# A convolution and a two-layer MLP on one core: the second tap sum from superblock 10 on, and a checked softmax with a general version behind it

## The chip, the cores and the metric

The kernel runs on one core of one Trainium2 chip. The time is that of the device in microseconds. Before the change it is 746.78 us, the median of three runs (745.8 to 747.22).

The core's engines are named as in the profile: PE (TensorE, matmuls), PEld (its weight loads), DVE (VectorE), ACT (ScalarE), POOL (GpSimd) and SP (SyncE, which here only issues DMAs).

## The reference

x is 8 x 4096 x 192 (float32), weight_gen is 8 x 4096 x 8 x 7, w_in is 192 x 2048 and w_out is 2048 x 192. A softmax over seven weights for each token and each of eight heads gives the taps of a causal convolution along the sequence. The result goes through a matmul, a tanh-shrink and a second matmul.

```
w = weight_gen - np.max(weight_gen, axis=-1, keepdims=True)
w = np.exp(w)
w = w / (np.sum(w, axis=-1, keepdims=True) + 1e-09)
...
out = np.einsum('bshk,bskhg->bshg', w, x_unf)      # x_unf: tokens s-6 .. s
...
h = x @ w_in
g = h - np.tanh(h)
return (g @ w_out).astype(np.float32)
```

## The kernel before

The 32768 tokens are cut into 32 superblocks of 1024, numbered 0 to 31. Partition p of a superblock holds the eight consecutive tokens 8p to 8p + 7. One superblock passes these stages, spread over the time of several superblocks:

- **Softmax, four superblocks ahead.** SP loads the weights (L120), ACT takes the exponential in place without subtracting a maximum (L169), DVE sums it in two halves (`softmax_sum`, L183), takes the reciprocal (L198) and scales (L229). From superblock 28 on there is none of this left to do.
- **Taps, two superblocks ahead.** POOL multiplies x by the seven taps (L299). Taps 0 to 3 go to the tile `pa` in two instructions, taps 4 to 6 to `pb` in one. `products` issues the first, and `rest` the `pb` product at f = 3 or later. DVE takes over taps 0 and 1 of the last token of each partition, and in superblocks 9 to 14 of the last two tokens (`HELP`, the function `help`, L250 and L251). An entry (n, f) of `HELP[m]` says that DVE works for superblock m in superblock n after f tile f.
- **Tap sums by DMA.** A DMA that adds (L236, issued by POOL) adds `pb` to taps 0 to 2 of `pa`. That leaves four parts. For a superblock in `TWO_SUMS`, a second such DMA adds taps 2 and 3 of `pa` to taps 0 and 1, which leaves two. `second_sum` issues it after the first products of the next superblock.
- **Transposes, one superblock ahead.** PE transposes and adds up the remaining parts in PSUM against an identity (L384), 24 matmuls for each part, and ACT copies the result to `convT` (L410).
- **First matmul, f = 0 to 15.** Six matmuls for each of 16 tiles of 128 hidden units (L427) into a PSUM tile `ph`, of which there are three buffers. ACT takes the tanh (L440), and DVE subtracts it and writes `gt` (L441), which frees `ph`.
- **Second matmul, one superblock behind.** `out_stream` (L495) works through token blocks in pairs of matmuls, ACT copies each block to `out_sb` (L514), and SP stores a superblock at a time (L518). The last superblock has its own version, `gemm2_last` (L538), with an ACT copy (L551), a DVE add (L552) and a store for two blocks (L554).

The order on each engine is the order of the program text (a manual schedule). A plan fixes, for each superblock, how many pairs of the second matmul follow each f tile (`pairs`), and behind which tile the two transposes stand (`t1` for chunk 2, `t2` for chunks 0 and 1). `DOUBLE` has the larger transposes behind f = 11 and the smaller behind f = 15, `STEADY` behind f = 13 and 14:

```
STEADY = dict(pairs=(5, 11, 0, 16, 4, 12, 6, 10, 0, 6, 10, 8, 8, 8, 8, 16), t1=(14, 8), t2=(13, 0), scale=14, sums=(1, 13))
...
DOUBLE = dict(pairs=(4, 12, 0, 16, 0, 16, 5, 11, 0, 5, 11, 6, 10, 0, 16, 16), t1=(15, 4), t2=(11, 4), scale=15, sums=(1, 10))
DOUBLE_IN = (4, 5, 6, 7, 8, 9, 10, 11)
```

So superblock n with the plan `DOUBLE` transposes superblock n + 1. On SP, the load of x for superblock m is ordered behind the first product of superblock m - 1 on POOL (from superblock 10 on), and everything behind it in the queue of SP waits too.

## Time and profile before

| | |
|---|---|
| Median of three runs | 746.78 us (745.8 to 747.22) |
| Span of the profiled execution | 743.4 us; its whole time is not listed |
| Granted clock of PE, mean | 0.995 |
| PE, busy | 722.3 us (97%) |
| DVE, busy | 687.4 us (92%) |
| POOL, busy | 654.5 us (88%) |
| ACT, busy | 638.8 us (86%) |
| Chain that ended last | PE 92%, DVE 5% |
| Superblock 9 / superblock 15 | 22.67 us / 21.86 us |
| Landing of a first tap sum / a second, median | 9.5 us / 7.2 us |

Times inside the profile count from the start of its span. Busy time counts an engine's own work; a DMA-issuing instruction of POOL or SP is listed under the engine that issues it. In lists by time the first number is the start, the second the length; the bracket at the end gives the idle time before it and what ended that.

### The profile page before, as it was taken

What the parts mean: (1) busy time and instruction counts of PE and PEld (TensorE: products, weight loads), DVE (VectorE), ACT (ScalarE), POOL (GpSimd) and SP (SyncE); (2) the same over time, 40 slices, a digit from 0 to 9 for tenths busy, and PEclk for the clock granted to TensorE, in tenths of its full rate; (3) what the DMA queues carried; (4) which work ended last, traced back from release to release, by engine and by line L of the source; (5) the groups of instructions that cost most, each with busy time, mean ns of one, the idle gap of its engine ahead of it and who ended that gap; (6) DMA issues with size and microseconds to landing.
All of it is one profiled execution on the core that took longest, in us unless ns stands there. A gap on an engine that the chain in (4) does not pass through costs nothing.

```text
span 743.4 us, 30037 instructions
## 1 busy us (share of the span) xinstructions
PE 722.3 (97%) x13616; PEld 556.5 (75%) x13616; DVE 687.4 (92%) x723; ACT 638.8 (86%) x872; POOL 654.5 (88%) x163
## 2 busy tenths in 40 slices
PE   3899999999999999999999999999999999999997
PEld 2477777778777777777777777777777777877777
DVE  7999899999999999999999999999999999988893
ACT  4888888888888888989889999898998989888882
POOL 7999999999999999999999999999999999991000
PEclk9899999999999999999999999999999999999999
DMA  8925367766567668878777977877887877776112
GB/s 236 245 46 161 135 172 185 195 179 149 124 183 184 183 185 224 210 199 203 166 202 209 236 186 204 178 195 205 221 209 195 192 181 194 193 149 110 45 45 86
DMA packets 34269, 130.06 MB, mean 175 GB/s; under 512 B 4591, under 2 KB 9439, under 8 KB 30174
## 3 DMA queue, kind: packets, MB, share of 16 engines
q0 software_dynamic: 19424, 51.12, 40.4%
q1 hardware_dynamic: 14718, 77.03, 27.6%
q8 instruction: 106, 1.74, 0.9%
q14 instruction: 21, 0.17, 0.1%
HBM read 54.52 MB, written 25.17 MB: 107 GB/s over the span
## 4 chain that ended last, share of the span: by engine, by line
PE 92%; DVE 5%; ACT 1%; issue 1%; DMA 1%; SPq 0%; DVEq 0%
PE ph L427 43%; PE obank L495 43%; PE pc L384 4%; DVE gt L441 3%; PE po L538 1%; ACT th L440 1%; DVE pa L299 1%; DMA wg_t<-in_weight_gen_dram 1%; DVE zsum L183 0%; SPq L134 0%; ACT convT L402 0%; DVE obank L211 0%; DVE pa L251 0%; DVE pb L299 0%; SPq L144 0%
## 5 line engine op out<-in xcount | busy, mean ns | idle before, releaser
L441 DVE TENSOR_TENSOR gt<-ph,th 128x1024 bf16<-128x1024 f32 x512 | 601.6, 1217 | 33.4 <-ACT th L440 23.2
L440 ACT ACTIVATE th<-ph 128x1024 f32<-128x1024 f32 x512 | 512.1, 1025 | 69.2 <-PE ph L427 60.3
L427 PE MATMUL ph<-convT,w_in 64*128 64x512 bf16 x3072 | 415.1, 379 | 5.3 <-DVE gt L441 3.3
L495 PEld LDWEIGHTS <-gt 64*128 64x128 bf16 x7936 | 355.6, 94 | 80.6 <-issue 6.3
L495 PE MATMUL obank<-w_out,gt 64*128 64x192 bf16 x7936 | 408.0, 243 | 0.9 <-issue 0.8
L299 POOL TENSOR_TENSOR pa<-x_t,wsm 128x2688 bf16<-128x2688 f32 (+3 forms) x68 | 338.9, 5232 | 0.2
L299 POOL TENSOR_TENSOR pb<-x_t,wsm 128x4608 bf16<-128x4608 f32 (+2 forms) x33 | 283.8, 8601 | 0.7 <-ACT wsm L221 0.5
L427 PEld LDWEIGHTS <-w_in 64*128 64x128 bf16 x3072 | 163.0, 94 | 86.0 <-issue 18.3
L514 ACT ACTIVATE out_sb<-obank 128x192 f32<-128x192 f32 x248 | 81.3, 328 | 11.2 <-PE obank L495 10.3
L410 ACT ACTIVATE convT<-pc 128x1024 bf16<-128x1024 f32 (+1 forms) x62 | 50.1, 810 | 2.9 <-PE pc L384 2.7
L236 POOL DMA_DIRECT2D pa<-pb x28 | 36.0, 1284 | 13.7 <-POOL pb L299 9.1
L384 PEld LDWEIGHTS <-pa 64*128 64x128 bf16 x2064 | 41.5, 100 | 6.8 <-DVE pa L299 1.1
L236 POOL DMA_DIRECT2D pa<-pa x21 | 34.7, 1651 | 9.6 <-DMA pa<-pb 8.9
L384 PE MATMUL pc<-ident,pa 64*128 64x64 bf16 x1968 | 41.2, 191 | 1.8 <-POOL pa L299 0.9
L183 DVE TENSOR_REDUCE zsum<-wg_t 128x32 f32<-128x224 f32 (+1 forms) x61 | 23.6, 387 | 2.9 <-ACT wg_t L169 2.9
L169 ACT ACTIVATE wg_t<-wg_t 128x448 f32<-128x448 f32 x32 | 18.2, 570 | 6.3 <-DMA wg_t<-in_weight_gen_dram 6.2
L251 DVE TENSOR_TENSOR pa<-x_t,ph 128x384 bf16<-128x384 f32 x34 | 18.8, 554 | 2.0 <-DVE ph L250 0.3
L229 DVE TENSOR_TENSOR wsm<-wg_t,pc 128x448 f32<-128x448 f32 x27 | 16.8, 621 | 2.5
L198 DVE RECIPROCAL pc<-zsum 128x64 f32<-128x64 f32 x27 | 14.9, 550 | 0.0
L384 PE MATMUL pc<-ident,pb 64*128 64x64 bf16 x216 | 4.9, 206 | 9.0 <-POOL pb L299 9.0
L384 PEld LDWEIGHTS <-pb 64*128 64x128 bf16 x288 | 6.3, 106 | 9.5 <-POOL pb L299 9.0
L538 PE MATMUL po<-w_out,gt 64*128 64x192 bf16 x256 | 11.2, 243 | 0.0
(27 smaller groups left out, 56.8 us busy)
## 6 DMA issues: line engine op xcount, KB each, us to landing
x_t<-in_x_dram SPq DMA_DIRECT2D x31, 1344.0 KB, 7.9
pa<-pb POOLq DMA_DIRECT2D x28, 1152.0 KB, 9.5
out_dram<-out_sb SPq DMA_DIRECT2D x31, 768.0 KB, 3.9
pa<-pa POOLq DMA_DIRECT2D x21, 768.0 KB, 7.2
wg_t<-in_weight_gen_dram SPq DMA_DIRECT2D x32, 224.0 KB, 7.1
x_t<-in_x_dram SPq DMA_DIRECT2D x1, 768.0 KB
w_out<-in_moe_w_out_dram POOLq DMA_DIRECT2D x1, 768.0 KB, 9.5
out_dram<-out_sb SPq DMA_DIRECT2D x4, 192.0 KB, 3.0
```

The source lines that it names most:

```text
L183: nc.vector.reduce_sum(out=zsum_of[n][:, j0 * H : j1 * H], in_=e_of[n][:, j0:j1].rearrange("p j h k -> p (j h) k"), axis=AX.X,)
L236: return nc.gpsimd.dma_start(out=out.rearrange("p k j d -> p k (j d)"), in_=in_.rearrange("p k j d -> p k (j d)"), accum_op=mybir.AluOpTyp ...
L251: nc.vector.tensor_mul(pa[:, 0:KH, j, :].rearrange("p k (h g) -> p k h g", h=H), bass.AP(tensor=x_v.tensor, offset=x_v.offset + j * D, ap= ...
L299: return eng.tensor_mul(prod(k0, k1)[:, :, j0:j1].rearrange("p k j (h g) -> p k (j h) g", h=H), bass.AP(tensor=x_v.tensor, offset=x_v.offs ...
L384: nc.tensor.matmul(pc[r][:, col : col + R] if home else pc[:, r, col : col + R], lhsT=prods[c][gi][r * R : (r + 1) * R, 2 * j : 2 * j + 2] ...
L410: last_conv[0] = nc.scalar.activation(out=out, in_=pc[:, :, 0:cols].rearrange("p r (cj t) -> p r cj t", t=R), func=ACT.Copy,)
L427: nc.tensor.matmul(ph[:, r, :], lhsT=w_in[r * R : (r + 1) * R, c, f * P : (f + 1) * P], rhs=convT[r * R : (r + 1) * R, c, :], start=(c == ...
L440: last_act[0] = nc.scalar.activation(out=th[:], in_=ph_f, func=ACT.Tanh)
L441: last_sub[0] = nc.vector.tensor_sub(gt[:], ph_f, th[:])
L495: mm = nc.tensor.matmul(po[:, 0:D], lhsT=g_of[n][f][r * R : (r + 1) * R, col : col + P], rhs=w_out[r * R : (r + 1) * R, f, :], start=(r == ...
L514: last_act[0] = nc.scalar.activation(out=out_sb[:, j, :], in_=po[:, 0:D], func=ACT.Copy)
L538: nc.tensor.matmul(po[:, r, 0:D], lhsT=g_of[n][f][r * R : (r + 1) * R, col : col + P], rhs=w_out[r * R : (r + 1) * R, f, :], start=(f == 0 ...
```

## The change

The change has three parts.

1. Superblocks 10, 11 and 12 join `TWO_SUMS`, and `DOUBLE_IN` ends at 8, so superblocks 9, 10 and 11 follow the plan `STEADY`.
2. `HELP` loses the second token of superblocks 12, 13 and 14. POOL's first product for them has 2688 columns in place of 2304.
3. All softmax sums are kept in one tile, `zall`. DVE takes the largest and the smallest of each half of it (in superblocks 28 to 31), compares them with 1e30 and 1e-18, and reduces the outcome to one integer, after a DMA has brought the 128 partitions' answers into one row. Every engine loads that integer and branches. If a sum was out of range, a general version in loops (with the maximum subtracted) computes everything anew. The store of the last two token blocks stands behind the branch, on both ways.

```
-    TWO_SUMS = (13, 14, 15, ... 31)
+    TWO_SUMS = (10, 11, 12, 13, 14, 15, ... 31)
...
-    HELP = {...} | {9: ((7, 3), (6, 12)), 10: ((8, 3), (7, 12)), 11: ((9, 3), (8, 12)), 12: ((10, 3), (9, 12)), 13: ((11, 3), (10, 12)), 14: ((12, 3), (11, 12))}
+    HELP = {...} | {9: ((7, 3), (6, 12)), 10: ((8, 3), (7, 12)), 11: ((9, 3), (8, 12))}
...
+    STORES = {1: 0, 3: 2, 5: 4}
+    LAST_STORE = {7: 6}
+    SUM_MAX, SUM_MIN = 1e30, 1e-18
+    CHECK = {(28, 14): (0,), (29, 14): (1,), (30, 14): (2,), (31, 8): (3,)}
...
-            zsum_of[n] = wgpool.tile([P, J * H], FP32, name="zsum")
+            zsum_of[n] = zall[:, n * J * H : (n + 1) * J * H]
...
+    def sums_piece(i):
+        w = NTOT * J * H // 2
+        if i < 4:
+            op = ALU.max if i < 2 else ALU.min
+            nc.vector.tensor_reduce(ends[:, i : i + 1], zall[:, i % 2 * w : (i % 2 + 1) * w], AX.X, op)
+        elif i == 4:
+            nc.vector.tensor_scalar(ends[:, 0:2], ends[:, 0:2], SUM_MAX, None, op0=ALU.is_le)
+        elif i == 5:
+            nc.vector.tensor_scalar(ends[:, 2:4], ends[:, 2:4], SUM_MIN, None, op0=ALU.is_ge)
+        elif i == 6:
+            nc.vector.tensor_mul(fine[:], ends[:, 0:2], ends[:, 2:4])
+            nc.sync.dma_start(out=fine_row[:], in_=fine[:])
+        else:
+            nc.vector.tensor_reduce(flag[:], fine_row[:], AX.X, ALU.min)
...
-        if j % 2 == 1:
-            nc.sync.dma_start(...)
+        if j in STORES:
+            store_last(j)
...
-    DOUBLE_IN = (4, 5, 6, 7, 8, 9, 10, 11)
+    DOUBLE_IN = (4, 5, 6, 7, 8)
...
+            for piece in CHECK.get((n, f), ()):
+                sums_piece(piece)
...
+    for piece in (4, 5, 6):
+        sums_piece(piece)
     gemm2_last(0, 0, J)
     out_pairs(NFT)
     gemm2_last(0, J, NFT)
     for j in range(1, J):
+        if j == 4:
+            sums_piece(7)
         gemm2_last(j)
+    sched.__exit__(None, None, None)
...
+    good = nc.values_load(flag[:], min_val=0, max_val=1)
+    with tc.If(good < 1, preferred_fallthrough_block=False):
+        with tc.For_i(0, B) as b:
+            carry = xpool.tile([P, HALO + J, D], FP32, name="x_t")
+            nc.vector.memset(carry[0:1, 0:HALO, :], 0.0)
+            with tc.For_i(0, NSB) as s:
+                general(b * NSB + s, carry)
+    STORES.update(LAST_STORE)
+    store_last(J - 1)
```

`general` (not shown) does one superblock from the loads to the store. With the inputs of the reference every sum is in range, and it is never entered.

More of the change, by code (lines that the diff above doesn't have):

```diff
@@ L13 @@
 AX = mybir.AxisListType
+ALU = mybir.AluOpType
 @with_exitstack
@@ L45 @@
     PART = (2, 3)
-    TWO_SUMS = (13, 14, 15, 16, 17, 18, 19, 20, 21, 22, 23, 24, 25, 26, 27, 28, 29, 30, 31)
+    TWO_SUMS = (10, 11, 12, 13, 14, 15, 16, 17, 18, 19, 20, 21, 22, 23, 24, 25, 26, 27, 28, 29, 30, 31)
     AHEAD = 4
@@ L49 @@
     EXTRA = (5, 9, 11, 13)
-    HELP = {n: ((n - 2, 3),) for n in (4, 5, 6, 7, 8, 9, 10, 11, 12, 13, 14, 15, 16, 17, 18, 19, 20, 21, 22, 23, 24, 25, 26, 27, 28, 29, 30, 31)} | {9: ((7, 3), (6, 12)), 10: ((8, 3), (7, 12)), 11: ((9, 3), (8, 12)), 12: ((10, 3), (9, 12)), 13: ((11, 3), (10, 12)), 14: ((12, 3), (11, 12))}
+    HELP = {n: ((n - 2, 3),) for n in (4, 5, 6, 7, 8, 9, 10, 11, 12, 13, 14, 15, 16, 17, 18, 19, 20, 21, 22, 23, 24, 25, 26, 27, 28, 29, 30, 31)} | {9: ((7, 3), (6, 12)), 10: ((8, 3), (7, 12)), 11: ((9, 3), (8, 12))}
     LAST_TAP = (4, 5, 6, 7, 8)
     X_LATE = ()
+    STORES = {1: 0, 3: 2, 5: 4}
+    LAST_STORE = {7: 6}
+    SUM_MAX, SUM_MIN = 1e30, 1e-18
+    CHECK = {(28, 14): (0,), (29, 14): (1,), (30, 14): (2,), (31, 8): (3,)}
     ZERO_AT = 8
@@ L83 @@
     once = const.tile([P, 1], FP32, name="once")
+    zall = const.tile([P, NTOT * J * H], FP32, name="zall")
+    ends = const.tile([P, 4], FP32, name="ends")
+    fine = const.tile([P, 2], FP32, name="fine")
+    fine_row = const.tile([1, 2 * P], FP32, name="fine_row")
+    flag = const.tile([1, 1], mybir.dt.int32, name="flag")
     x_of = {}
@@ L197, in softmax_norm @@
         zr_v = bank[:, 512 - J * H : 512]
-        nc.vector.reciprocal(zr_v, zsum_of[n][:])
+        nc.vector.reciprocal(zr_v, zsum_of[n])
         def finish():
@@ L210, in softmax_norm_ramp @@
         zr_v = bank[:, 512 - J * H : 512]
-        nc.vector.reciprocal(zr_v, zsum_of[n][:])
+        nc.vector.reciprocal(zr_v, zsum_of[n])
         if n == 2:
@@ L527, in out_pairs, with store_last @@
             next(pairs)
+    def store_last(j):
+        n = NTOT - 1
+        nc.sync.dma_start(
+            out=out[n * TOK : (n + 1) * TOK, :].rearrange("(p j) e -> p j e", p=P)[:, STORES[j] : j + 1, :],
+            in_=out_of[n][:, STORES[j] : j + 1, :],
+        )
     def gemm2_last(j, f0=0, f1=NFT):
@@ L552, in gemm2_last @@
         nc.vector.tensor_add(out_sb[:, j, :], po[:, 1, 0:D], ot[:])
-        if j % 2 == 1:
-            nc.sync.dma_start(
-                out=out[n * TOK : (n + 1) * TOK, :].rearrange("(p j) e -> p j e", p=P)[
-                    :, j - 1 : j + 1, :
-                ],
-                in_=out_sb[:, j - 1 : j + 1, :],
-            )
+        if j in STORES:
+            store_last(j)
     w_in = const.tile([P, NC, F], BF16, name="w_in")
     w_out = const.tile([P, NFT, D], BF16, name="w_out")
-    ctx.enter_context(tc.manual_schedule())
+    sched = tc.manual_schedule()
+    sched.__enter__()
     def load_w_out():
@@ L773, with general, rows, spread @@
     for j in range(1, J):
+        if j == 4:
+            sums_piece(7)
         gemm2_last(j)
+    sched.__exit__(None, None, None)
+    def general(m, carry):
+        x_t = xpool.tile([P, HALO + J, D], FP32, name="x_t")
+        def rows(p0, p1, r0, r1):
+            first = x.rearrange("b s d -> (b s) d")[bass.ds(m * TOK, 1)]
+            nc.sync.dma_start(
+                out=x_t[p0:p1, r0:r1, :],
+                in_=bass.AP(
+                    tensor=first.tensor,
+                    offset=first.offset + (p0 * J - HALO + r0) * D,
+                    ap=[[J * D, p1 - p0], [D, r1 - r0], [1, D]],
+                ),
+            )
+        rows(0, P, HALO, HALO + J)
+        rows(1, P, 0, HALO)
+        nc.sync.dma_start(out=x_t[0:1, 0:HALO, :], in_=carry[0:1, 0:HALO, :])
+        nc.sync.dma_start(out=carry[0:1, 0:HALO, :], in_=x_t[P - 1 : P, J : J + HALO, :])
+        e_t = wgpool.tile([P, J, H, K], FP32, name="wg_t")
+        nc.sync.dma_start(
+            out=e_t[:],
+            in_=weight_gen.rearrange("b s h k -> (b s) h k")[bass.ds(m * TOK, TOK)].rearrange(
+                "(p j) h k -> p j h k", p=P
+            ),
+        )
+        e_v = e_t[:].rearrange("p j h k -> p (j h) k")
+        zr = wgpool.tile([P, J * H], FP32, name="zr")
+        def spread(v):
+            return v.rearrange("p (n o) -> p n o", o=1).to_broadcast([P, J * H, K])
+        nc.vector.tensor_reduce(zr[:], e_v, AX.X, ALU.max)
+        nc.vector.tensor_sub(e_v, e_v, spread(zr[:]))
+        nc.scalar.activation(
+            out=e_t[:].rearrange("p j h k -> p (j h k)"),
+            in_=e_t[:].rearrange("p j h k -> p (j h k)"),
+            func=ACT.Exp,
+        )
+        nc.vector.reduce_sum(out=zr[:], in_=e_v, axis=AX.X)
+        nc.vector.reciprocal(zr[:], zr[:])
+        nc.vector.tensor_mul(e_v, e_v, spread(zr[:]))
+        total = papool.tile([P, J, D], FP32, name="total", tag="pa")
+        part = papool.tile([P, J, D], FP32, name="part", tag="pa")
+        summed = pbpool.tile([P, J, D], BF16, name="pb")
+        x_v = x_t[:]
+        for k in range(K):
+            to = total if k == 0 else part
+            nc.vector.tensor_mul(
+                to[:].rearrange("p j (h g) -> p (j h) g", h=H),
+                bass.AP(tensor=x_v.tensor, offset=x_v.offset + k * D, ap=[x_v.ap[0], [G, J * H], [1, G]]),
+                e_t[:].rearrange("p j h (k o) -> p k (j h) o", o=1)[:, k].to_broadcast([P, J * H, G]),
+            )
+            if k > 0:
+                nc.vector.tensor_add((summed if k == K - 1 else total)[:], total[:], part[:])
+        prods_of[NTOT] = [[summed[:]]] * NC
+        conv(NTOT, (0, 1), (2,))
+        convT = conv_of.pop(NTOT)
+        out_sb = opool.tile([P, J, D], FP32, name="out_sb")
+        nc.vector.memset(out_sb[:], 0.0)
+        with tc.For_i(0, NFT) as f:
+            w_f = tpool.tile([P, NC, P], BF16, name="w_f", tag="th")
+            nc.sync.dma_start(out=w_f[:], in_=w_in[:, :, bass.ds(f * P, P)])
+            w_o = tpool.tile([P, D], BF16, name="w_o", tag="th")
+            nc.sync.dma_start(out=w_o[:], in_=w_out[:, bass.ds(f, 1), :].rearrange("p o e -> p (o e)"))
+            ph = psum_h.tile([P, 2, HT], FP32, name="ph", tag="ph")
+            for c in range(NC):
+                for r in range(2):
+                    nc.tensor.matmul(
+                        ph[:, r, :],
+                        lhsT=w_f[r * R : (r + 1) * R, c, :],
+                        rhs=convT[r * R : (r + 1) * R, c, :],
+                        start=(c == 0),
+                        stop=(c == NC - 1),
+                    )
+            th = tpool.tile([P, TOK], FP32, name="th")
+            gt = gpool.tile([P, TOK], BF16, name="gt0", tag="gt0")
+            ph_f = ph[:].rearrange("p r t -> p (r t)")
+            nc.scalar.activation(out=th[:], in_=ph_f, func=ACT.Tanh)
+            nc.vector.tensor_sub(gt[:], ph_f, th[:])
+            for j in range(J):
+                po = psum_h.tile([P, 2, HT], FP32, name="po2", tag="ph")
+                col = (j % 2) * HT + (j // 2) * P
+                for r in range(2):
+                    nc.tensor.matmul(
+                        po[:, r, 0:D],
+                        lhsT=gt[r * R : (r + 1) * R, col : col + P],
+                        rhs=w_o[r * R : (r + 1) * R, :],
+                        start=True,
+                        stop=True,
+                    )
+                for r in range(2):
+                    nc.vector.tensor_add(out_sb[:, j, :], out_sb[:, j, :], po[:, r, 0:D])
+        nc.sync.dma_start(
+            out=out[bass.ds(m * TOK, TOK), :].rearrange("(p j) e -> p j e", p=P),
+            in_=out_sb[:],
+        )
+        (j,) = LAST_STORE
+        last = slice(LAST_STORE[j], j + 1)
+        nc.vector.tensor_copy(out_of[NTOT - 1][:, last, :], out_sb[:, last, :])
```

## The prediction

> **What bounds the kernel now.** I read the page first, for the busy shares and the chain that ended last, then the busy time by superblock, then the order of PE and of POOL in time, and the end last.

> ```profile
> span 743.4 us, 30037 instructions
> ...
> PE 722.3 (97%) x13616; PEld 556.5 (75%) x13616; DVE 687.4 (92%) x723; ACT 638.8 (86%) x872; POOL 654.5 (88%) x163
> ...
> PE 92%; DVE 5%; ACT 1%; issue 1%; DMA 1%; SPq 0%; DVEq 0%
> ```

> PE is 92% of the chain, so a matmul less inside a superblock is time less. But POOL and DVE are nearly as full, so whatever is moved onto them must be checked against the need of PE.

> Busy time in superblock 9 and in superblock 15 (PE, weight loads, DVE, ACT, POOL, then clock, DMA share and GB/s):

> ```profile
> 220.87:243.54 22.67, 22.67 (x453) 17.68 (x450) 21.60 (x25) 19.85 (x27) 22.37 (x6) 1.00 0.78 184
> ...
> 354.75:376.61 21.86, 21.86 (x406) 16.85 (x402) 21.04 (x23) 19.71 (x28) 21.14 (x6) 1.00 0.82 202
> ```

> PE is busy in every nanosecond of both. Superblock 9 has 453 matmuls, 15 has 406: the 47 or 48 between them (a record can be missing) are the transposes that the second tap sum saves, and they cost 0.81 us. PE in order of time (start, us, what): transposes of superblocks 9, 10, 13 and 14 at L384, and the first matmuls of superblocks 9 and 13 at L427.

> ```profile
> 213.01 1.11 PE L384 MATMUL pc<-ident,pa 64*128 64x64 bf16 x64
> ...
> 220.87 0.83 PE L427 MATMUL ph<-convT,w_in 64*128 64x512 bf16 x6
> ...
> 235.68 1.11 PE L384 MATMUL pc<-ident,pa 64*128 64x64 bf16 x64
> ...
> 306.00 0.65 PE L384 MATMUL pc<-ident,pa 64*128 64x64 bf16 x32
> ...
> 310.75 0.83 PE L427 MATMUL ph<-convT,w_in 64*128 64x512 bf16 x6
> ...
> 327.85 0.65 PE L384 MATMUL pc<-ident,pa 64*128 64x64 bf16 x32
> ```

> The period is 235.68 - 213.01 = 22.67 with four parts to transpose and 327.85 - 306.00 = 21.85 with two. In the STEADY plan the transposes begin 327.85 - 310.75 = 17.10 after the superblock's first matmul. POOL in order of time:

> ```profile
> 216.44 1.28 POOL L236 DMA_DIRECT2D pa<-pb  x1 [0.30 <-POOL pb L299]
> 217.26 10.33 POOL L299 TENSOR_TENSOR pa<-x_t,wsm 128x2304 bf16<-128x2304 f32 x2
> 227.06 8.83 POOL L299 TENSOR_TENSOR pb<-x_t,wsm 128x4608 bf16<-128x4608 f32 x1
> ...
> 297.18 1.28 POOL L236 DMA_DIRECT2D pa<-pb  x1 [0.77 <-DVE pa L251]
> 298.00 11.02 POOL L299 TENSOR_TENSOR pa<-x_t,wsm 128x2688 bf16<-128x2688 f32 x2
> 308.47 1.72 POOL L236 DMA_DIRECT2D pa<-pa  x1
> 309.24 9.32 POOL L299 TENSOR_TENSOR pb<-x_t,wsm 128x4608 bf16<-128x4608 f32 x1
> 319.04 1.28 POOL L236 DMA_DIRECT2D pa<-pb  x1 [0.47 <-POOL pb L299]
> ```

> The first sum at 216.44 is that of superblock 10, the one at 297.18 that of 14. POOL never rests: 19.75 us from one first sum to the next with one sum and two VectorE tokens (216.44 to 236.19), 21.86 with two sums and one token.

> **The second tap sum for 10, 11 and 12.** Their transposes stand in superblocks 9, 10 and 11, which also take the STEADY plan, as 13 and later do. Each goes from 22.67 to 21.85: 3 x 0.82 = 2.46 us less on PE. The bounds are a loss of nothing and the whole 2.46; a larger gain is excluded, since PE has no idle time there. I take 2.46, because the same plan runs at 21.86 in the second window shown.

> This holds only if the sums land in time. For superblock 10: POOL is unchanged up to 227.06, where the second sum is now issued (its first sum is down: 9.5 us from 216.44, the median of that row, gives 225.9). The row pa<-pa has a median of 7.2 us to landing, so 234.3. PE now asks for it at 220.87 + 17.10 = 237.97. That leaves 3.7 us, where superblock 14 has 327.85 - (308.47 + 7.2) = 12.2 today. Then POOL pays 319.04 - 308.47 = 10.57 to its next first sum (237.63), 0.8 for issuing and 10.47 for the two products, now with 2688 columns for superblocks 12, 13 and 14 (one token moved back from DVE; 10.47 against 9.80 is 0.67 each). So the second sums of 11, 12 and 13 are issued at 248.9, 270.8 and 292.6, land 7.2 later at 256.1, 278.0 and 299.8, and are wanted at 259.8, 281.7 and 303.5. The cover is 3.7 us throughout and does not shrink, since both periods are now 21.85. Behind each of the three added issues POOL's next product, its next first sum and, on SP, the load of x three superblocks on (ordered behind the first product) come later, about 6 us by superblock 14; that load lands some 20 us before its use, so it costs nothing. The DVE help that POOL waited for at 297.18 is then long done.

> If a sum came late, PE's transposes would wait, and later ones would not add to it, because the periods are equal: the price is once the lateness. The slowest landing among the sums is 10.9 us in the window from 210 to 340 us; that would still fit to within 0.0.

> **Fewer VectorE tokens.** Three copies of 190 ns and three products of 554 ns leave DVE, 2.2 us in all, beside PE's work: nothing gained.

> **Four reductions over the softmax sums.** The reduction L183 takes 375 ns for 224 elements and 614 for 448, so 1024 elements give 375 + 800 x 1.067 = 1.23 us each (bounds 0.6 and 2.5). Three stand at f = 14 of superblocks 28 to 30, where the reciprocal (0.55) and the scaling (0.62) stood before and are gone, since no softmax is left: same size, same place, no cost. The fourth stands in superblock 31, behind the subtraction of f = 8. There DVE has no slack:

> ```profile
> 718.49 7.18 DVE L441 TENSOR_TENSOR gt<-ph,th 128x1024 bf16<-128x1024 f32 x6 [0.25 <-ACT th L440]
> 721.22 0.83 PE L427 MATMUL ph<-convT,w_in 64*128 64x512 bf16 x6
> ```

> These six subtractions (f = 8 to 13, counted back from the last) are back to back, 1.14 us from start to start. PE's tile f = 12 at 721.22 takes the PSUM buffer that the subtraction of f = 9 frees at 718.49 + 1.14 + 1.22 = 720.85. The slack is 0.37; behind the reduction it is freed at 722.0 to 722.1, so PE stalls about 0.85. Bounds: nothing, and 1.23. I take 0.85, and DVE is level again by f = 15.

> **The end.** Three small DVE operations (190 ns, as the copy) and a DMA of 1 KB follow the last subtraction; the store of 192 KB takes 1.9 us from issue to landing at the end (740.36 to about 742.2), so the flag's row is there by some 733, before the reduction that stands ahead of block 4's add at 736. The reduction of 256 elements (0.41) fits in DVE's 0.96 us of idle time. Then every engine loads the flag and branches, and SP waits for all its earlier stores and only then issues the last one.

> ```profile
> 737.72 2.97 SPq L554 DMA_DIRECT2D out_dram<-out_sb  x2
> ...
> 739.97 0.36 DVE L552 TENSOR_TENSOR out_sb<-po,ot 128x192 f32<-128x192 f32 x1 [0.96 <-ACT ot L551]
> ```

> The third store, issued at 737.72, lands at about 737.72 + 1.9 = 739.6. The last may go at 740.36, so 0.7 us is left for the closing waits and two jumps. SP's closing jump and waits in the kernel before take under 0.45 (its wait for the last store is 1.1 us and ends near 742.2). The flag's load on PE, ACT and DVE runs beside the last store. [...]

> [...]

> **Sum.** -2.46 + 0.85 + 0.2 = -1.4 us. The profiled span of 743.4 becomes 742.0. The page gives no time of that execution but its span; the median of the three runs, 746.78, lies 3.4 above it, and I leave that unchanged: 745.4.

> **Rivals.**
> The check hides: superblock 31 absorbs the reduction. For it: DVE's idle time just before, 0.25, recurs; against it: the six back to back. -2.46 + 0.2 = -2.3, 744.5.

> The sums come late: the added sums share the DMA engines (78% busy in superblock 9) with the load of x and the store of out. For it: first sums take up to 10.9; against it: second sums have a median of 7.2. A landing of 10.9 to 13.4 for superblock 10 (lateness 0 to 2.5) gives 745.4 to 747.9; from 2.9 late it is slower than now.

> [...]

> That the change does not do what it says: PE might not be the limit of 9 to 11. DVE needs 21.04 and POOL 21.14 in the second window, both under 21.85, so this is the late case again.

> **How the numbers follow.** A measurement of this kernel tells some 0.2%, 1.5 us, from no change, so faster begins below 745.3. The forecast (0.55) sits at that edge: 0.30 faster, 0.25 same. The hidden check 0.12, faster. Late sums 0.13: 0.07 same, 0.06 slower. Branch 0.20: 0.10 same (one fetch), 0.10 slower. In all 0.42, 0.42, 0.16. The range runs from the hidden check's 744.5 less 0.4 for the spread of the runs, 744.1, to 748.2, short of two fetches; the forecast's own is 744.7 to 746.2.

> **What would show it.** Superblocks 9, 10 and 11 at 21.85 with 405 matmuls; the transposes of 10 with no wait for a DMA; second sums of 10 at 227.1; a PE gap of 0.8 at f = 12 of superblock 31; the last store issued within 0.1 us of the last DVE add. Wrong would be PE waiting at L410 for a tap sum, or more than a microsecond between that add and that store.

## The result and the profile after

The changed kernel takes 749.89 us (median of four runs, 749.49 to 750.32) against 746.29 us for the kernel before on the same chip (four runs, 745.68 to 747.22). The ratio is 1.0051, with a 95% interval of 1.0037 to 1.0065: it is slower by 3.6 us, where 1.4 us less was forecast.

The page of the changed kernel, the lines that answer to those shown of before, and three more:

```profile
span 748.0 us, 29794 instructions
...
PE 721.8 (96%) x13472; PEld 557.0 (74%) x13472; DVE 690.7 (92%) x725; ACT 638.9 (85%) x872; POOL 660.3 (88%) x166
...
q14 instruction: 26, 0.21, 0.1%
...
PE 92%; DVE 5%; issue 1%; ACT 1%; DMA 0%; DVEq 0%
...
L521 PE MATMUL obank<-w_out,gt 64*128 64x192 bf16 x7936 | 410.0, 243 | 3.9 <-issue 3.7
...
pa<-pa POOLq DMA_DIRECT2D x24, 768.0 KB, 9.3
```

The same three lines of the page of before (of these the prediction uses the 7.2 of the last):

```profile
q14 instruction: 21, 0.17, 0.1%
...
L495 PE MATMUL obank<-w_out,gt 64*128 64x192 bf16 x7936 | 408.0, 243 | 0.9 <-issue 0.8
...
pa<-pa POOLq DMA_DIRECT2D x21, 768.0 KB, 7.2
```

PE has 144 matmuls fewer, as planned, and is still the engine of the chain. What is new is small: PE idles 3.7 us ahead of second matmuls with "issue" as the end of the wait, which was 0.8 (L521 is the old L495, moved by the added lines). "Issue" means that PE waited for nothing that the profile shows. q14, a queue that the page lists as instructions, has five more 8 KB packets (26 for 21), and a second tap sum takes 9.3 us to land in place of 7.2 (medians of one execution each).

By place, from the start of each superblock's first matmul in the two profiled executions (a table of ours, differences worked out from the trace):

| | before | after | difference |
|---|---|---|---|
| superblocks 9 to 12 | 89.88 | 87.44 | -2.44 |
| superblocks 13 to 30 | 395.36 | 399.34 | +3.98 |
| superblock 31 to the end of its last DVE add | 34.22 | 35.02 | +0.80 |
| from there to the end of the span | 3.07 | 5.24 | +2.17 |

The rest of the difference of 4.6 in span is 0.1 before superblock 9. The profiled execution of before was a good one, 743.4: in the changed kernel's profiled execution the time is 1.9 above the span, and 1.7 to 2.1 in every run for which both are listed, so 743.4 stands for some 745.3, about 1.0 below the median of 746.29. The differences in the table are against that good execution.

**The gain came.** Busy time of the changed kernel in superblocks 9, 24 and 25 (PE, weight loads, DVE, ACT, POOL, then clock, DMA share, GB/s):

```profile
220.98:242.84 21.86, 21.86 (x405) 16.95 (x402) 21.06 (x23) 19.70 (x27) 21.56 (x6) 1.00 0.89 209
...
550.52:572.99 22.47, 21.99 (x406) 16.43 (x402) 21.03 (x23) 19.90 (x28) 21.68 (x6) 1.00 0.80 202
572.99:597.28 24.29, 22.25 (x406) 17.49 (x402) 22.22 (x25) 19.72 (x28) 23.99 (x7) 1.00 0.83 223
```

Superblock 9 is down from 22.67 to 21.86, all of it busy, with 405 matmuls. But superblock 25, far behind the change and with the same 406 matmuls as any other, takes 24.29, and PE is idle for 2.04 of it.

**It was given back in superblocks 13 to 30.** PE in order of time around the largest of these waits (start, length, what, idle time before):

```profile
568.24 0.65 PE L410 MATMUL pc<-ident,pa 64*128 64x64 bf16 x32
...
570.79 0.41 PE L410 MATMUL pc<-ident,pa 64*128 64x64 bf16 x16
...
573.64 0.24 PE L521 MATMUL obank<-w_out,gt 64*128 64x192 bf16 x1
574.94 0.57 PE L521 MATMUL obank<-w_out,gt 64*128 64x192 bf16 x9 [1.06 <-issue]
```

POOL in order of time, first where the added second sums stand, then at the time of that wait:

```profile
227.03 1.72 POOL L262 DMA_DIRECT2D pa<-pa  x1
227.81 9.32 POOL L325 TENSOR_TENSOR pb<-x_t,wsm 128x4608 bf16<-128x4608 f32 x1
237.42 1.28 POOL L262 DMA_DIRECT2D pa<-pb  x1 [0.30 <-POOL pb L325]
238.24 11.01 POOL L325 TENSOR_TENSOR pa<-x_t,wsm 128x2688 bf16<-128x2688 f32 x2
248.71 1.72 POOL L262 DMA_DIRECT2D pa<-pa  x1
...
563.73 1.28 POOL L262 DMA_DIRECT2D pa<-pb  x1 [0.79 <-DVE gt L467]
```

The first tap sum at 563.73 is issued 4.5 us ahead of the transposes at 568.24. The DMA queues from 566 to 572.5 us, while it runs, and then from 572.5 to 575 us (packets, MB, share of the 16 DMA engines):

```profile
q0 software_dynamic: 368, 1.08, 98.1%
q1 hardware_dynamic: 18, 0.19, 11.4%
```

```profile
q1 hardware_dynamic: 84, 0.90, 93.2%
q8 instruction: 1, 0.02, 2.4%
q0 software_dynamic: 1, 0.00, 0.1%
```

```
PE goes on   packet on q8 starts   between   the sum's packets ran
376.65       374.43                2.22      369.67 to 377.43
384.77       382.32                2.44      (382.14 to 389.23)
398.36       396.03                2.33      391.35 to 399.00
552.97       550.57                2.40      543.40 to 550.58
574.94       572.77                2.17      565.58 to 572.79
596.93       594.53                2.40      587.27 to 594.54
618.54       616.16                2.38      608.95 to 616.17
639.92       637.51                2.41      630.66 to 637.53
```

All eight waits end 2.2 to 2.4 us after the packet starts. In five, the packet starts in the very moment in which the sum ends; in two, some 4.7 us after the sum's first packet (a last packet or two of two sums come later and are left out of the table). The same pattern stands where PE does not run dry: beside each of the 21 first sums issued from superblock 9 on, one packet of q8 starts, 13 times within 0.3 us of the sum's end, 6 times 4.7 to 6.1 us after its first packet, twice in its first 1.6 us, and never in between.

The eighth wait (384.77) has no first sum ahead of it (the bracket gives a second sum, which begins as the packet starts): there q1, with the loads and stores that SyncE issues, has 96.8% of the DMA engines from 377 to 382 us. The larger of the two such waits of the kernel before (0.55, up to 378.30) is of that kind too: its packet starts at 375.92, the sum had ended at 371.99, and q1 has 88.2% from 372 to 375.9.

The 256 instructions ahead of the wait at 574.94 begin at 568.27, with the transposes, whose instructions are the shortest (32 matmuls of L410 start within 0.47 us, 16 of L521 within 0.77, six of L453 within 0.65): this line was used up in 5.4 us. Elsewhere in a superblock a line lasts up to 8 us by estimate (82 matmuls and 77 weight loads from 560.5 to 565.5, that is 159 in 5.0 us). Counted on in such lines from the waits (255.7 recorded instructions each), each of the 69 packets from superblock 9 on up to 704.72 starts 2.2 to 8.0 us before the first instruction of its line, and at all eight waits it is 2.2 to 2.4. So the reading, which the experiments test: PE runs dry where the sum's packets and the transposes fall together.

The list of idle times shows less than PE loses. The eight waits are 3.97 us together, where superblocks 13 to 30 take 6.0 more than 18 times the 21.855 of one without a wait. From the start of the last matmul ahead of a wait to the start of the first one behind it, the eight are 6.00 us (1.30 for the one of 1.06): a matmul of L521 is listed with 0.24 us, but 32 of them without a wait start 0.04 us apart.

What moved is the place of the first tap sum, counted from the first matmul of the superblock in which it is issued. In the kernel before it is 8.3 to 9.1 for superblocks 14 to 31, since POOL there waits for DVE's help (L251). After, it is 15.9 for superblock 14, 13.5 for 20, 12.9 for 25, and back at 8.3 for 31: POOL issues the sum of 14 at 302.5 in place of 297.2, 5.3 later, and PE starts superblock 12 2.3 earlier. POOL's period of 21.68 is a little shorter than PE's 21.86, and that and PE's waits then use up the difference.

**The fourth reduction and the end.** PE at f = 12 of superblock 31, then DVE at the same time:

```profile
722.22 0.84 PE L521 MATMUL obank<-w_out,gt 64*128 64x192 bf16 x16
723.68 0.82 PE L453 MATMUL ph<-convT,w_in 64*128 64x512 bf16 x6 [0.62 <-DVE gt L467]
```

```profile
721.29 1.21 DVE L204 TENSOR_REDUCE ends<-zall 128x1 f32<-128x1024 f32 x1
722.41 5.74 DVE L467 TENSOR_TENSOR gt<-ph,th 128x1024 bf16<-128x1024 f32 x5
```

The tile starts 15.91 after the superblock's first matmul; before, 15.11. The last stores and the last add (the prediction shows those of before), and what SyncE waits for at the end, after and then before:

```profile
737.53 6.58 SPq L557 DMA_DIRECT2D out_dram<-out_sb  x3
...
742.43 0.36 DVE L585 TENSOR_TENSOR out_sb<-po,ot 128x192 f32<-128x192 f32 x1 [0.96 <-ACT ot L584]
```

```profile
SPq L950 <- DMA out_dram<-out_sb: 1.8, 1, 1.8
```

```profile
SPq L800 <- DMA out_dram<-out_sb: 1.1, 1, 1.1
```

SyncE's own records give the rest of the 2.17. Its branch ends at 742.58, and its next instruction starts at 743.69. The last store is issued at 743.78, 0.99 after the last add, where before needed 0.03: 0.96 more. From its issue to its landing as SyncE sees it are 2.80, against 1.87 before: 0.93 more. The closing is 0.27 longer. The DMA queues from 743.6 to 746.7 us:

```profile
q1 hardware_dynamic: 144, 0.20, 22.2%
q14 instruction: 3, 0.02, 3.1%
```

Three 8 KB packets on q14 (743.80 to 744.93) and a 16 KB one on q8 (743.40 to 744.56) run just ahead of the store's own 144 packets and into them; before, none does. The store's packets begin 0.84 after the issue, as before (0.82), but take 1.49 from the first to the last in place of 0.68. In e4 (below) the store leaves later, its packets begin as the last of four on q14 ends, and they take 0.65, with 1.96 from issue to landing. So the instruction packets beside it go with the slower landing; that they cause it was not tested. Which engine each packet on q14 belongs to is not in the records.

### The profile page after: what moved, and what is told of

It is laid out like the page before. It is cut to its first block, busy times and chain, and to the rows that moved or that the text cites. A ratio compares the mean times of both kernels' runs of the same rounds, so it can differ in the third digit from the quotient of the medians.

```text
span 748.0 us, 29794 instructions
## 1 busy us (share of the span) xinstructions
PE 721.8 (96%) x13472; PEld 557.0 (74%) x13472; DVE 690.7 (92%) x725; ACT 638.9 (85%) x872; POOL 660.3 (88%) x166
## 4 chain that ended last, share of the span: by engine, by line
PE 92%; DVE 5%; issue 1%; ACT 1%; DMA 0%; DVEq 0%
PE ph L453 43%; PE obank L521 43%; PE pc L410 4%; DVE gt L467 2%; PE po L571 1%; ACT th L466 1%; DVE pa L325 1%; DVE pb L325 0%; DMA wg_t<-in_weight_gen_dram 0%; DVE zall L193 0%; DVE obank L237 0%; PE obank L410 0%; DVE wsm L255 0%; DVE obank L255 0%; ACT wg_t L179 0%
## 5 line engine op out<-in xcount | busy, mean ns | idle before, releaser
L453 PE MATMUL ph<-convT,w_in 64*128 64x512 bf16 x3072 | 417.4, 379 | 5.7 <-DVE gt L467 3.7
L521 PEld LDWEIGHTS <-gt 64*128 64x128 bf16 x7936 | 356.9, 94 | 84.4 <-issue 11.6
L521 PE MATMUL obank<-w_out,gt 64*128 64x192 bf16 x7936 | 410.0, 243 | 3.9 <-issue 3.7
L453 PEld LDWEIGHTS <-w_in 64*128 64x128 bf16 x3072 | 165.0, 94 | 84.1 <-issue 19.0
L540 ACT ACTIVATE out_sb<-obank 128x192 f32<-128x192 f32 x248 | 81.4, 328 | 12.4 <-PE obank L521 11.5
L262 POOL DMA_DIRECT2D pa<-pa x24 | 39.7, 1656 | 9.7 <-DMA pa<-pb 9.1
L410 PEld LDWEIGHTS <-pa 64*128 64x128 bf16 x1920 | 39.9, 101 | 6.8 <-DVE pa L325 1.0
L410 PE MATMUL pc<-ident,pa 64*128 64x64 bf16 x1824 | 39.4, 192 | 1.6 <-DVE pa L325 0.7
L193 DVE TENSOR_REDUCE zall<-wg_t 128x32 f32<-128x224 f32 (+1 forms) x61 | 23.6, 387 | 2.8 <-ACT wg_t L179 2.8
L224 DVE RECIPROCAL pc<-zall 128x64 f32<-128x64 f32 x27 | 14.9, 550 | 0.0
L410 PE MATMUL pc<-ident,pb 64*128 64x64 bf16 x216 | 4.9, 206 | 9.0 <-POOL pb L325 9.0
L410 PEld LDWEIGHTS <-pb 64*128 64x128 bf16 x288 | 6.3, 107 | 9.5 <-POOL pb L325 9.0
L571 PE MATMUL po<-w_out,gt 64*128 64x192 bf16 x256 | 11.2, 243 | 0.0
```

Of the source, the lines that this page charges most:

```text
L193: nc.vector.reduce_sum(out=zsum_of[n][:, j0 * H : j1 * H], in_=e_of[n][:, j0:j1].rearrange("p j h k -> p (j h) k"), axis=AX.X,)
L262: return nc.gpsimd.dma_start(out=out.rearrange("p k j d -> p k (j d)"), in_=in_.rearrange("p k j d -> p k (j d)"), accum_op=mybir.AluOpTyp ...
L410: nc.tensor.matmul(pc[r][:, col : col + R] if home else pc[:, r, col : col + R], lhsT=prods[c][gi][r * R : (r + 1) * R, 2 * j : 2 * j + 2] ...
L453: nc.tensor.matmul(ph[:, r, :], lhsT=w_in[r * R : (r + 1) * R, c, f * P : (f + 1) * P], rhs=convT[r * R : (r + 1) * R, c, :], start=(c == ...
L521: mm = nc.tensor.matmul(po[:, 0:D], lhsT=g_of[n][f][r * R : (r + 1) * R, col : col + P], rhs=w_out[r * R : (r + 1) * R, f, :], start=(r == ...
L540: last_act[0] = nc.scalar.activation(out=out_sb[:, j, :], in_=po[:, 0:D], func=ACT.Copy)
```

## The experiments

Times are medians beside runs of the kernel before on the same chip; "excess" is what superblocks 13 to 30 take beyond 18 x 21.855 us in the profiled execution, and "first sum" its place for superblock 14, in us from the first matmul of superblock 12. Excess is that of one execution, and executions differ: the ten of e11 run from 743.79 to 749.26.

| run | time | before | ratio (95%) | excess | first sum |
|---|---|---|---|---|---|
| kernel before | | | | 2.0 | 8.3 |
| changed kernel | 749.89 | 746.29 | 1.0051 (1.0037 to 1.0065) | 6.0 | 15.9 |
| e6_after_again, the same | 750.11 | 746.65 | 1.0050 (1.0033 to 1.0066) | 6.3 | 15.8 |
| e1_sums_only | 745.15 | 745.93 | 0.9987 (0.9972 to 1.0002) | 3.1 | 16.1 |
| e13_sums_again, the same | 745.71 | 745.69 | 1.0005 (0.9995 to 1.0015) | 2.9 | 15.9 |
| e2_check_only | 748.79 | 745.93 | 1.0037 (1.0025 to 1.0050) | 2.6 | 8.3 |
| e3_tokens_kept | 749.92 | 745.93 | 1.0048 (1.0031 to 1.0066) | 3.0 | 11.4 |
| e4_no_stores, one run | 750.83 | | | 6.0 | 15.8 |
| e9_no_first_sums, one run | 744.28 | | | 0.3 | none |
| e18_pool_later | 749.25 | 745.54 | 1.0049 (1.0034 to 1.0063) | 6.0 | 15.6 |
| e5_shift | 752.62 | 746.65 | 1.0087 (1.0067 to 1.0107) | 6.6 | 13.8 |
| e12_before_pad64 | 749.85 | 745.69 | 1.0055 (1.0040 to 1.0070) | 0.8 | 8.3 |
| e10_sums_pad90 | 747.93 | 745.69 | 1.0033 (1.0021 to 1.0044) | 4.1 | 14.3 |
| e11_sums_pad32 | 746.59 | 745.69 | 1.0008 (0.9991 to 1.0025) | 5.6 | 15.7 |
| e8_end_mended | 748.76 | 746.65 | 1.0029 (1.0017 to 1.0040) | 5.9 | 15.9 |
| e16_one_superblock | 745.18 | 745.54 | 0.9991 (0.9979 to 1.0002) | 1.1 | 10.5 |
| e17_two_superblocks | 747.05 | 745.54 | 1.0024 (1.0015 to 1.0032) | 5.1 | 13.3 |

**Each part alone.** e1_sums_only is the kernel before with `TWO_SUMS` from 10, `DOUBLE_IN` up to 8 and `HELP` without the three second tokens. e2_check_only is the changed kernel with these three lines as they were:

```
-    TWO_SUMS = (10, 11, 12, 13, ... 31)
+    TWO_SUMS = (13, ... 31)
...
-    DOUBLE_IN = (4, 5, 6, 7, 8)
+    DOUBLE_IN = (4, 5, 6, 7, 8, 9, 10, 11)
```

> The sums, the tokens and the plan of the change, without the check, the branch and the general version. Theory (late instructions: PE stands still in superblocks 16, 17 and 24 to 28 because its next 16 KB of instructions come late behind the tap sums' DMAs): the same stalls as in the changed kernel, start of superblock 31 at 707.7 in the profile (706.1 before), no stall in 31 and the old end: 746.3 + 1.6 = 747.9. Rival (the check and its code cost throughout): superblocks 12 to 30 as before, 746.3 - 2.4 = 743.9.

> The check, the branch and the general version on the old sums, tokens and plan. Theory: superblocks as before, a stall of 0.8 in superblock 31 and 2.1 more at the end: 746.3 + 2.9 = 749.2. Rival (the check costs throughout): superblocks 16, 17 and 24 to 28 are longer here too, some 753.

The check costs 2.9, as expected once the traces had been compared: f = 12 of superblock 31 at 15.91, the last store at 743.12 behind a branch that ends at 741.61, superblocks 9 to 12 within 0.4 us of before. The sums and plans alone, on which the forecast put -2.46, are worth 0.8 in one run, between the two times expected, and nothing in the other; both ratios include 1. The two parts add up to some 2.5 and the whole is 3.5, so the changed kernel takes about 1 us more than its parts. The same programs again (e13, e6) show that the waits keep their sum but not their places:

> The sums, tokens and plan without the check, once more, beside padded forms of it on one chip. 0.5 to 1.5 us below the kernel before, with 3 to 5 us of stalls left between superblocks 13 and 30.

> The changed kernel once more, beside the parts on one chip. If the parts add up (the sums -0.8, the check +2.9): 2.1 above the kernel before, some 748.0. If they act on each other through PE's instruction fetches: 3.6 above, some 749.5, with stalls in superblocks 16, 17 and 24 to 28 of 5 us or more together, where the sums alone had 3.8.

e1 waits in superblocks 23 to 26 and e13 in 24 to 26; the changed kernel in 14 to 17 and 24 to 28, its repetition in 15 to 20. e13 was expected 0.5 to 1.5 faster than the kernel before and is not; e6 measures the time expected if the parts act on each other.

**What holds PE: three suspects.** e3 gives DVE the second tokens back, e4 leaves out the stores of the output of superblocks 13 to 27 (these rows are not written), e9 leaves out the first tap sums of superblocks 13 to 27 (taps 4 to 6 are missing from them).

```
e3:  HELP = ... | {9: ..., 10: ..., 11: ..., 12: ((10, 3), (9, 12)), 13: ((11, 3), (10, 12)), 14: ((12, 3), (11, 12))}
e4:  +            if n not in range(13, 28):
                      nc.sync.dma_start(       # the store of out_sb
e9:  +                if n not in range(13, 28):
                          dma_sum(pa[:, 0:3], pb[:, 0:3])
```

> The changed kernel with the second VectorE tokens of superblocks 12, 13 and 14 kept. POOL is 2 us earlier from superblock 14 on, and each second sum has 2 us more before its transposes. Theory (the tap sums' place in time against PE's instruction fetches decides): the stalls change place or size; if they shrink with POOL's lead, 748.0 to 749.0. Rival (POOL's lead does not matter): 749.9 as the changed kernel, within 0.4.

> The changed kernel without the stores of superblocks 13 to 27 (those rows of the output are left out), everything else as it is. Theory (the instruction fetches wait behind a DMA load made of tap sum, load of x and store): second sums land in 8 us instead of 9.3 to 10.5, and the stalls of 14 to 28, 5.9 us together, fall under 2.5: one time near 746.5. Rival (the stalls come from something on PE itself, or from the sums alone): 5.9 us of stalls remain, 749.9.

> The changed kernel without the first tap sums (pb into pa) of superblocks 13 to 27, so their taps 4 to 6 are left out of the result. Theory (the sums hold up PE's instruction fetches): no stall over 0.3 us in superblocks 14 to 27, superblock 31 starts at 702.5 to 703.5 in place of 707.8, the time is near 745. Rival (loads of x and second sums suffice, or PE itself stalls): stalls of 3 us or more remain in 14 to 28.

e3 measures 749.92, the time of its rival. That is not because the place does not matter: e3 brings the first sums nearer to their old place, and excess falls from 6.0 to 3.0; but superblocks 9 to 11 lose their gain (22.75, 22.73, 22.73), because DVE's second token now stands in the way of the smaller plan. PE in superblock 10 of e3:

```profile
261.22 0.84 PE L521 MATMUL obank<-w_out,gt 64*128 64x192 bf16 x16
262.87 0.82 PE L453 MATMUL ph<-convT,w_in 64*128 64x512 bf16 x6 [0.81 <-DVE pa L277]
```

So the change of `HELP`, for which the prediction saw no more than idle time on DVE, is needed for the gain. e4 missed its expectation. Its second sums do land sooner: those issued between 357 and 554 us take 6.8 to 8.2 us without a store beside them, where the changed kernel's take 8.5 to 10.5. (The median of a whole run does not tell this: it is 7.3 in e4, and 7.3 in e6 with its stores, where the sums are back near their old place sooner.) But PE waits in the same superblocks as in the changed kernel, with the same excess. e9 has none of the waits. Busy time of e9 from 302 to 324 and from 564 to 586 us:

```profile
302.00:324.00 22.00, 22.00 (x410) 16.98 (x406) 21.19 (x23) 19.86 (x28) 22.00 (x5) 1.00 0.49 147
564.00:586.00 22.00, 22.00 (x410) 16.99 (x406) 21.18 (x24) 19.85 (x28) 14.70 (x3) 1.00 0.34 92
```

PE is busy throughout, every superblock from 13 to 27 takes 21.85 to 21.87, and superblock 31 starts at 702.48 in place of 707.77. The first tap sums are the cause. The second sums, the loads of x and the stores are still there, and they alone do not make PE wait here. That DMA share falls by half shows a load, not yet a place, which the next run tells.

**The place alone.** e18 is the kernel before, with POOL put back by two repeated products and nothing changed for PE, DVE or the end (POOL's second sums and, behind its products, the loads of x move with the first sums):

```
+        if n == 14:
+            mul(nc.gpsimd, 0, KH, 0, J - nt)
+            mul(nc.gpsimd, 0, KH, 0, 4)
         first = mul(nc.gpsimd, 0, KH, 0, J - nt)
```

> The kernel before, with two more products on POOL ahead of those of superblock 14 (they write values that the next product writes again, so the result is the same). They take some 8.1 us, of which 0.77 is POOL's idle time, so from superblock 14 on the first tap sums are issued some 15.6 us after the first matmul of the superblock they stand in, not 8.3, and drift back by 0.17 us a superblock. PE's instructions are those of before. Theory (the place of the first tap sums starves PE's instruction fetch): superblocks 13 to 30 are longer by 2 to 5 us in all, at idle stretches on L495 that end with "issue"; 748 to 751 us. Rival (the place is without effect, the stalls come from the changed plans, the check or the code behind it): no change, 745.7 +- 0.8.

749.25, inside the expected 748 to 751: 3.7 us slower, with an excess of 6.0, that of the changed kernel. The first sums stand at 15.6 for superblock 14, 14.9 for 18, 11.4 for 20 and 9.6 for 25. POOL and PE in e18 around its longest wait:

```profile
370.33 1.30 POOL L236 DMA_DIRECT2D pa<-pb  x1 [0.55 <-DVE gt L444]
```

```profile
374.96 0.41 PE L387 MATMUL pc<-ident,pa 64*128 64x64 bf16 x16
...
377.81 0.49 PE L498 MATMUL obank<-w_out,gt 64*128 64x192 bf16 x7
379.80 0.32 PE L498 MATMUL obank<-w_out,gt 64*128 64x192 bf16 x3 [1.50 <-issue]
```

The packet that PE waits for starts at 377.32, 5.1 us after the sum's first one. No check, no branch and no changed plan is in this kernel. To move POOL's work is enough to lose what the changed kernel lost in superblocks 13 to 30, and e9 says that it takes the first tap sums.

**The place of the line boundaries.** If PE runs dry at the end of a line of 256 instructions, instructions that do nothing must move the waits. Each of these kernels has small matmuls into an unused PSUM tile, once, ahead of the first transposes (64 in e5 and e12, 90 in e10, 32 in e11):

```
+    pad = psum_h.tile([P, 2, HT], FP32, name="pad", tag="ph")
+    for _ in range(64):
+        nc.tensor.matmul(pad[0:R, 0, 0:R], lhsT=ident[0:R, 0:R], rhs=ident[0:R, 0:R], start=True, stop=True)
```

e5 is the changed kernel so shifted, e12 the kernel before, e10 and e11 the sums alone.

> The changed kernel with 64 extra matmuls (128 instructions, half a 16 KB line) on PE ahead of the first transposes, where PE waits for its data; their result is not used. Theory (late instructions: a line asked for while a tap sum fills the DMA engines comes when the sum ends, and PE stands still if it has used up the line before): the boundaries of the lines move by half a line, about three superblocks, so the stalls leave 16, 17 and 24 to 28 and stand mainly in 9 to 12 and 20 to 23; total between 2 and 8 us, so 747 to 752. Rival (the superblock's own work stalls PE): the stalls stay in 16, 17 and 24 to 28, 749.5.

> The kernel before with 64 unused matmuls (128 instructions) ahead of the first transposes. Theory (late instructions): the kernel before has its stalls by the chance of where its lines begin; they move, and the time goes up by 0.5 to 3 us or, if the place is luckier, down by up to 2. Rival: the same time as the kernel before within 0.3 us.

> The same with 90 unused matmuls (180 instructions) on PE before its first data is there, which costs no time by itself. From the sums' times and the lines' boundaries of the run without pads I estimate half the stalls: theory (late instructions) 1 to 3 us below the unpadded form, so 2 to 4 us below the kernel before; the stalls stand in other superblocks. Rival (the boundaries do not matter): the time of the unpadded form within 0.5 us.

> The same with 32 unused matmuls (64 instructions). The estimate in the same way is two thirds of the stalls: 0.5 to 2 us below the unpadded form. Rival: the time of the unpadded form within 0.5 us.

The waits move with the boundaries: in e5 to superblocks 9 to 16 and 24 to 25, in e10 to 11, 12 and 18 to 22. Where they go was not foreseen in any of the four; e5 and e12 are slower than the range expected of them, and e10 and e11 were expected to be faster than the form without pads and are not. The plainest is e12: 64 matmuls, after which superblock 9 starts at 221.55 (220.59 to 222.18 in the other kernels), cost 4.2 us. Superblocks 9 to 12 alone take that much more (23.50, 23.51, 24.66 and 22.42 in place of 22.67, 22.68, 22.67 and 21.86), while 13 to 30 take 1.2 less. PE of e12 in superblock 11:

```profile
285.94 0.38 PE L427 MATMUL ph<-convT,w_in 64*128 64x512 bf16 x1
288.25 1.04 PE L427 MATMUL ph<-convT,w_in 64*128 64x512 bf16 x8 [1.94 <-issue]
```

The packet of that line starts at 285.97, and the sum ahead of it ends there. So the kernel before has a lucky place of its boundaries in these superblocks, where its own first sums still come late (15.3 for superblock 11, 12.4 for 12), and excess between the three kernels with the sums alone runs from 2.9 to 5.6. The 1 us that the changed kernel has more than its parts lies within that, but that its boundaries are the reason was not shown; it stays open.

**The end.** e8 moves the fourth reduction behind the last subtraction, issues the third store a block earlier and so lets SyncE take the branch before the last add; the last store then holds three blocks.

```
-    STORES = {1: 0, 3: 2, 5: 4}
-    LAST_STORE = {7: 6}
+    STORES = {1: 0, 3: 2, 4: 4}
+    LAST_STORE = {7: 5}
-    CHECK = {(28, 14): (0,), (29, 14): (1,), (30, 14): (2,), (31, 8): (3,)}
+    CHECK = {(28, 14): (0,), (29, 14): (1,), (30, 14): (2,)}
...
-    for piece in (4, 5, 6):
+    for piece in (3, 4, 5, 6):
```

> The changed kernel with its fourth reduction moved behind the last subtraction of superblock 31, and the third store made after block 4 (one block), the last one for blocks 5 to 7. Theory: the stall of 0.8 in superblock 31 goes, and SP passes its jump (1.1 us without an instruction) before the last add, so the last store is issued within 0.1 us of it, 0.9 sooner: 1.7 less than the changed kernel, 747.8 if that has 749.5. Rival (the last store is late by the branch itself): only the 0.8 goes.

It gains 1.35 on the changed kernel's repetition on the same chip (750.11), of 1.7 expected. The stall of superblock 31 is gone (f = 12 at 15.11), which is 0.80. The branch still takes 0.9 on SyncE (740.55 to 741.48) but ends early. The store yet leaves 0.42 after the last add, because SyncE then waits for DVE, which has a branch of its own, and it lands 3.06 after its issue in place of 2.80, with half as much again to carry. SyncE's waits in e8:

```profile
SPq L950 <- DMA out_dram<-out_sb: 2.1, 1, 2.1
...
SPq L557 <- DVEq L917: 0.8, 1, 0.8
```

**Smaller moves.** e16 and e17 change one and two superblocks in place of three, without the check:

```
e16: TWO_SUMS = (12, 13, ...)        DOUBLE_IN = (4, ... 10)    second tokens up to 13
e17: TWO_SUMS = (11, 12, 13, ...)    DOUBLE_IN = (4, ... 9)     second tokens up to 12
```

> The kernel before with the second tap sum from superblock 12 on, the plan DOUBLE up to 10, and the second VectorE token up to superblock 13: one superblock changed in place of three, no check. Superblock 11 goes from 22.67 to 21.85, a gain of 0.82. The first tap sum of 14 moves from 8.3 to some 9.8 us after its superblock's first matmul. Theory: that is short of the stretch from 12 to 17 in which the stalls were seen, so the gain is kept: 744.9, 0.9989. Rival (any move of the sums or the instruction lines costs what it gains): 745.7 +- 0.5.

> The same with superblocks 11 and 12 (second tap sum from 11 on, DOUBLE up to 9, second VectorE token up to 12). Superblocks 10 and 11 go from 22.67 to 21.85, a gain of 1.64. The first tap sums move to some 12 us after their superblock's first matmul, the edge of the stretch with stalls. Theory: part of the gain is given back, 0.8 of it: 744.9 +- 0.6. Rival (all of it is given back): 745.7 +- 0.5.

e16 measures 745.18 where 744.9 was expected, but the expected reason is not what its trace shows. With first sums at 10.5 and 11.2 PE does wait, in superblocks 11 and 12 (22.43 and 22.92), and the gain is given back there and more (9 to 12 take 90.70, before 89.88); what makes it no slower is an excess of only 1.1 later on. Its ratio includes 1. e17 missed: 747.05, slower by 1.5 with an excess of 5.1, though its first sums stand at 13.3 and not 16. No kernel with the whole result that was run beats the kernel before beyond its interval.

## Why the prediction was wrong

- **The 2.46 on superblocks 9 to 11: right.** They take 21.86 each, with 405 matmuls, and superblocks 9 to 12 together 2.44 less.
- **The step that failed** is in the working of the second tap sum: that POOL's first sums, its products and the load of x come "about 6 us" later and that this "costs nothing". It priced the load of x only. The first sum's own packets moved too, 5.3 us later on POOL while PE came 2.3 earlier, from 8.3 to some 16 us after the superblock's first matmul, to just ahead of the transposes; and the DMA engines that they fill (98.1% of 16 from 566 to 572.5 us) also move the packets of q8 (0.9% over the span). The cost is 4.0 us in superblocks 13 to 30 against the profile of before. e9 (without first sums, none of it) and e18 (POOL's work moved and nothing else, all of it) show this. The prediction looked for a wait of PE for a tap sum and named no wait of PE for its own instructions; the page of before had it in one line, 0.8 us with "issue" ahead of L495.
- **Landing of second sums: mis-sized.** 7.2 was taken from the row; superblocks 10 to 13 took 10.8, 10.6, 10.3 and 10.1. The cover of 3.7 was used up to 0.2 in superblock 9 (landed 237.81, wanted 237.97 by the prediction's own clock). The rival "the sums come late" did not decide: superblock 9 is at 21.86. The row's sums stand some 20 us after a superblock's first matmul, the added ones 5.5 to 6.1. The store of the output counts there: at 2 to 5 us sums take 8.5 to 10.5 with it and 6.8 to 8.2 without (e4).
- **Fewer VectorE tokens: right that nothing is gained by the idle time, wrong as a reading**; e3 shows that without this edit superblocks 9 to 11 keep 22.7.
- **The fourth reduction: right.** 1.21 us (1.23 taken), and 0.80 on PE (0.85); the rival in which it hides did not come.
- **The end: mis-sized**, 2.17 for 0.2. The 0.2 was the author's estimate, and no run shows it; the runs show the 2.17. The row used, 0.45 for closing waits and a jump to the next instruction, was no measure of a branch across the general version. The terms are 0.96 for the issue of the last store, 0.93 for a slower landing (which the prediction left as it was), 0.27 for the closing. The 0.20 of chance for the branch, and the fetches counted with it and in the range, are the author's estimate too. What the traces show is 1.11 us from the branch to the next instruction on SyncE and five more packets on q14 (26 for 21); that the 1.11 is a fetch was not shown.
- **From span to median: the wrong point to start from.** 3.4 was carried over, which is to take the 1.4 off the median of the three runs. On medians of one chip the step is +3.6 in place of -1.4, missed by 5.0 us, not the 4.5 that 749.89 lies above 745.4. Between the two profiles it is +4.6, missed by 6.0: 4.0 from superblocks 13 to 30, 2.0 from the end. The two differ because the profile of before lies some 1.0 below its median; where a run at the median loses that 1.0 was not shown, so the 4.0 may be nearer to 3 for such a run.

## What to carry to other kernels

Here, with PE 97% busy, tap sums issued 5.3 us later cost 4.0 us in superblocks 13 to 30, and the packets of PE's own instructions were what came late beside them. Where an engine is as full, look for idle time that ends with "issue", and see which DMA fills the queues there. A price of zero for "later by 6 us" needs the list of everything that will run beside it at the new place. And time a change next to a version with a few idle instructions added: here 128 instructions that do nothing cost 4.2 us (e12), more than the change could win.

## What the runs showed of the hardware

- While a first tap sum by DMA runs (98.1% of 16 engines' time from 566 to 572.5 us), a 16 KB packet on q8 started only when the sum ended (within 0.02 us, five times) or 4.7 us after its first packet (twice), in seven of the eight waits of the changed kernel from superblock 13 on; PE goes on 2.2 to 2.4 us after the packet's start in all eight, and 2.5 in the longest wait of e18 (377.32 to 379.80). In the eighth it is q1 that has the engines (96.8%). PE's idle time at such a wait is listed with up to 1.06 us in the changed kernel, 1.50 in e18 and 1.94 in e12.
- PE uses up 256 instructions in 5.3 to 5.8 us ahead of five of these waits and in 6.2 to 7.5 ahead of the others, and in about 8 from 560.2 to 568.3 us. The same delay is free in one place and a stall in the other: packets that start as a first sum ends are followed by no wait at 485.25 and 506.93, where the line's first instruction comes 4.3 and 3.8 us later, and by one at 550.57 and 572.77.
- A branch over the general version takes 0.9 to 1.4 us on SyncE until the next instruction in seven profiled executions (1.11 in the changed kernel, 1.42 in e2, 0.93 in e8) and 2.52 in e4, though nothing in between is executed.
- The store of 192 KB at the end lands in 2.80 us in place of 1.87 when instruction packets run beside its first packets, and in 1.96 in e4, where they are through by then.
